# Attention and two MLP layers on one core: other PSUM banks and another order of the weight work at the passage and the seams, and operands at SBUF addresses that are multiples of 512 bytes

## The chip, the cores and the metric

The kernel runs on one core of a Trainium2 chip. Times are device microseconds of an execution. The kernel before took 595.28 us, the median of three runs (594.83 to 597.52).

## The reference

Three stages follow each other. The first is a linear attention with decay, for 2 batches, 8 heads, 768 positions and 64 dimensions a head, by blocks of 64 positions. Its output, as 1536 tokens of 512 numbers, goes through two MLPs with hidden width 2048. All inputs are float32.

```
for b in range(nb):                       # blocks of 64 positions
    intra = (qb @ kb.T * Dmask) @ vb      # Dmask[i, j] = lam ** (i - j) for i >= j, else 0
    inter = (qb * lam_pow) @ kv_state
    out[:, :, sl] = intra + inter
    kv_state = lam_block * kv_state + (kb * rev_pow).T @ vb
h = x @ w_in1;  x = (h * cos(h)) @ w_out1
h = x @ w_in2;  x = (h / (1 + exp(-h))) @ w_out2
```

## The kernel before

**Numbers.** TensorE's matmuls take float32 values rounded to its fp32r form. To keep float32's precision each operand is split into an upper half (`xah`, `gh`, the first half of `win` and `wout`) and a lower half that holds the rest (`xal`, `gl`, the second half), and three matmuls are added: upper by upper, lower weight by upper, upper by lower. `split` (line 120) makes the halves: ScalarE casts the upper one, GpSimd (or the engine given) subtracts it from the value. Weights are read as raw integers, re-biased on ScalarE (`rebias_w`), converted on VectorE (`convert_w`, two instructions), and then split.

**Stages.** Attention runs in chunks of 128 positions (c = 0 to 5) and leaves x transposed: part A holds 512 tokens of each batch, as 2 by 2 quarters with their sums and differences (seven units), part B the rest. Each layer L then has a first product (x by `w_in`, with the nonlinearity) and a second (g by `w_out`), with the intermediate g written to memory (`gd`) and read back.

**First products.** The columns of the weights are taken in pairs j = 0 to 7. For a pair, `sum_w` forms four sums and differences of the weights on GpSimd (VectorE for the second layer's pairs 0 and 1), `split_plain` splits the weights themselves and `split_sums` the sums, and seven products of 6 matmuls (`PRODUCTS`, `product`, line 416) stand for eight. They add up in three PSUM banks: two of `two_banks(i)` (a, b) and one of `one_bank(i)` (d). ScalarE copies bank a to b (`copy_ab`) and b to SBUF (`copy_u`), VectorE forms the other two quarters (`c22`, `c21`). PSUM has eight banks: three pairs `two_banks(0)` to `(2)` and two single ones. In the first layer (`gemm_in_0`, line 510) part A's quads use bank pairs 0 and 1 in turn and part B is a plain product of 24 matmuls with 512 columns (`plain`, line 438) in bank pair 2. In each round j of its loop, TensorE does A's pair j and B's pair j - 1, and the weights of pair j + 1 are prepared by tasks (`task(j, 0)` to `(j, 2)`). In the second layer (`gemm_in_1`, line 577) both parts are quads, B with 256 columns, in bank pairs 2, 0, 1, 2, ..., and tasks are numbered by half a quad.

**Second products.** `gemm_outs` (line 782) walks over items (b, f): b is the block of 512 tokens, f one of 16 slices of the hidden width. One item is 12 matmuls of 512 columns (four output tiles m, three of the split). Blocks 0 and 1 run side by side, block 1 two slices behind, then block 2. Two output tiles of block 0 (m = 0, 1) for f = 0 and 1 are computed within the first product's end, as (0, 1). `load_g` reads g, `prepare` splits it.

**Order.** Each engine executes its instructions in the order of the program, which is written by hand; so does SyncE's queue of loads and stores. A pool's buffer is taken again when its last reader is done.

**Counts from the code.** Matmuls with 512 columns: 2 x 48 x 12 = 1152 in the second products, 2 x 8 x 42 = 672 for part A, 8 x 24 = 192 for part B of the first layer; with 256 columns 8 x 42 = 336 for part B of the second.

**Addresses.** Pools without a side are laid from the bottom of a partition's memory, pools with side "right" from its top. Below the first pool lie 16,512 bytes of the program's own (32 x 512 + 128); `consts` takes 512 and `zeros` 1,024, every later tile a multiple of 512, so that x of part A, g, all weights and all temporaries on the left start at a multiple of 512 plus 128. The right side ends at 229,344 (447 x 512 + 480), and its tiles (q, k, later x of part B, `xbh` and `xbl`) start at a multiple of 512 plus 480. The gap between both sides is 352 bytes. Within a tile, an operand's slices step by 1,024 or 2,048 bytes (x, g) or 512 (weights).

## Time and profile before

| | |
|---|---|
| median of 3 runs | 595.28 us (594.83 to 597.52) |
| profiled execution, in all | 592.26 us |
| its span, first to last instruction | 590.5 us |
| mean granted TensorE clock | 0.99 of 2.4 GHz |
| TensorE busy | 564.3 us (96%) |
| GpSimd, VectorE, ScalarE busy | 350.9, 347.8, 295.7 us |
| attention, to about 55 us | TensorE busy 50.1 of 55.0 us |
| passage and first round, 55 to 93 us | 33.6 of 38.0 |
| first layer, first product, 93 to 182.5 us | 89.4 of 89.5 |
| seam to the second product, 182.5 to 211 us | 20.0 of 28.5 |
| first layer, second product, blocks 0 and 1, to 288.5 us | 77.5 of 77.5 |
| its block 2, to 336 us | 46.6 of 47.5 |
| second layer, first product, to 454.5 us | 114.8 of 118.5 |
| second layer, second product, to 585 us | 130.5 of 130.5 |

A matmul is drawn for longer than the time until the next one starts, since they are pipelined; so a busy TensorE says that it isn't idle, not that it is at its best. Starts are to be read for that.

### The profile page before, as it was taken

The page shows a single profiled execution, that of the slowest core. Times are in us where ns is not written, and L with a number is a line of the kernel's source. Part 1 is how long each engine was busy: PE and PEld are TensorE (multiplying, and loading weights), DVE is VectorE, ACT ScalarE, POOL GpSimd, SP SyncE. Part 2 cuts the span into 40 slices and gives each one's busy share as a digit, 9 for nine tenths or more (in the row PEclk, how much of TensorE's full clock was granted, in tenths as well). Part 3 has the DMA queues.
Part 4 walks back from the last instruction along what each step waited for, and adds up shares of the span by engine and source line. Part 5 has one row for each costly group of instructions (what it writes and reads, how often), then busy time and mean ns, then how long its engine had stood idle before and what let it go on. Part 6 is the DMA issues. An engine that isn't in the chain of part 4 may idle for free.

```text
span 590.5 us, 8374 instructions
## 1 busy us (share of the span) xinstructions
PE 564.3 (96%) x3168; PEld 464.3 (79%) x3168; DVE 347.8 (59%) x355; ACT 295.7 (50%) x440; POOL 350.9 (59%) x261
## 2 busy tenths in 40 slices
PE   7999799999997699999999999999799999999997
PEld 4888587777776488888888788888689888888885
DVE  6689257776677599900499246667666799302001
ACT  4566267777776655310571365666656665201220
POOL 2688635555553699940489338555754699911541
PEclk9999999999998889999999999999999999999999
DMA  9999145445445886740044026455466896205501
GB/s 177 210 233 240 37 141 178 158 153 178 160 166 195 282 329 238 246 144 0 1 143 144 1 72 236 162 182 190 157 241 226 299 319 198 71 1 196 182 15 72
DMA packets 79640, 97.02 MB, mean 164 GB/s; under 512 B 40688, under 2 KB 57072, under 8 KB 79600
## 3 DMA queue, kind: packets, MB, share of 16 engines
q1 hardware_dynamic: 77360, 95.96, 50.8%
q10 hardware_dynamic: 2240, 0.53, 0.5%
q8 instruction: 25, 0.41, 0.3%
q14 instruction: 15, 0.12, 0.1%
HBM read 68.16 MB, written 28.31 MB: 163 GB/s over the span
## 4 chain that ended last, share of the span: by engine, by line
PE 72%; DVE 9%; POOL 6%; issue 4%; DMA 3%; ACT 3%; SPq 1%; ACTq 0%; DVEq 0%; POOLq 0%
PE cab L703 30%; PE cab L429 20%; PE d L429 8%; PE d L703 7%; PE cab L445 6%; DVE xal L122 2%; DVE S L134 2%; POOL win L122 2%; DVE sb L115 1%; DMA q<-in_q_dram 1%; DVE w L116 1%; ACT s L486 1%; DMA v<-in_v_dram 1%; POOL S L134 1%; DMA gf<-gd 1%
## 5 line engine op out<-in xcount | busy, mean ns | idle before, releaser
L122 POOL TENSOR_TENSOR gl<-gf,gh 128x512 fp32r<-128x512 f32 (+1 forms) x68 | 128.6, 1898 | 97.0 <-ACT gh L121 73.3
L703 PE MATMUL cab<-gh,wout 128*128 128x512 f32 x320 | 100.3, 395 | 2.4 <-ACT gh L121 2.4
L703 PE MATMUL cab<-wout,gh 128*128 128x512 f32 x320 | 98.6, 390 | 0.0
L121 ACT CAST gh<-gf 128x512 fp32r<-128x512 f32 (+1 forms) x68 | 53.5, 795 | 85.9 <-DMA out_dram<-o 29.3
L116 DVE SCALAR_TENSOR_TENSOR w<-w,sb 128x512 uint32<-128x512 uint32 x64 | 90.1, 1408 | 9.5 <-ACT w L106 3.2
L429 PE MATMUL cab<-xah,win 128*128 128x512 f32 x320 | 86.9, 394 | 0.2 <-ACT cab L459 0.2
L703 PEld LDWEIGHTS cab<-gh,wout 128*128 128x128 f32 x320 | 61.2, 191 | 15.6 <-ACT gh L121 2.8
L134 POOL TENSOR_TENSOR S<-w 128x256 f32<-128x256 f32 x28 | 30.6, 1091 | 69.6 <-DVE w L116 69.6
L703 PEld LDWEIGHTS cab<-wout,gh 128*128 128x128 f32 x320 | 59.9, 188 | 12.1
L429 PEld LDWEIGHTS cab<-xah,win 128*128 128x128 f32 x320 | 58.9, 188 | 12.8 <-ACT cab L459 0.6
L703 PE MATMUL cab<-gl,wout 128*128 128x512 f32 x160 | 63.7, 398 | 3.9 <-POOL gl L122 3.9
L122 POOL TENSOR_TENSOR wout<-w,wout 128x512 fp32r<-128x512 f32 x32 | 51.4, 1612 | 21.1 <-ACT wout L121 21.1
L115 DVE TENSOR_SCALAR sb<-raw 128x512 uint32<-128x512 uint32 x64 | 61.0, 954 | 3.0 <-DMA raw<-in_moe_w_out_dram 2.0
L703 PE MATMUL cab<-wout,gl 128*128 128x512 f32 x160 | 62.3, 389 | 0.0
L122 POOL TENSOR_TENSOR win<-S,win 128x512 fp32r<-128x512 f32 x32 | 46.5, 1474 | 7.6 <-ACT win L121 7.6
L429 PE MATMUL cab<-xal,win 128*128 128x512 f32 x160 | 49.5, 391 | 0.0
L466 ACT COPY u<-cab 128x512 f32<-128x512 f32 (+1 forms) x48 | 24.6, 513 | 46.9 <-PE cab L429 46.9
L778 DVE COPY o<-cab 128x512 f32<-128x512 f32 x10 | 6.7, 689 | 67.7 <-PE cab L703 65.3
L106 ACT ACTIVATE w<-raw 128x512 f32<-128x512 f32 x64 | 41.9, 671 | 7.3 <-POOL wout L122 3.4
L429 PE MATMUL d<-xah,win 128*128 128x512 f32 x128 | 36.9, 400 | 5.7 <-POOL win L122 2.7
L703 PEld LDWEIGHTS cab<-gl,wout 128*128 128x128 f32 x160 | 30.6, 191 | 11.5 <-POOL gl L122 5.3
L504 DVE TENSOR_TENSOR s<-cab,s 128x1024 f32<-128x1024 f32 (+1 forms) x32 | 34.7, 1084 | 7.0 <-ACT s L486 5.5
(125 smaller groups left out, 976.4 us busy)
## 6 DMA issues: line engine op xcount, KB each, us to landing
gf<-gd SPq DMA_DIRECT2D x46, 512.0 KB, 4.6
gd<-s SPq DMA_DIRECT2D x40, 512.0 KB, 3.1
raw<-in_moe_w_in_dram SPq DMA_DIRECT2D x32, 512.0 KB, 4.3
raw<-in_moe_w_out_dram SPq DMA_DIRECT2D x32, 512.0 KB, 4.6
gd<-s SPq DMA_DIRECT2D x16, 256.0 KB, 2.1
v<-in_v_dram SPq DMA_DIRECT2D x12, 256.0 KB, 6.3
out_dram<-o SPq DMA_DIRECT2D x12, 256.0 KB, 2.1
k<-in_k_dram SPq DMA_DIRECT2D x6, 256.0 KB, 5.7
```

The costliest lines, as they stand in the source:

```text
L106: nc.scalar.activation(w, raw[piece][:, :, 1].bitcast(F32), AF.Prelu, scale=2.0**-112, alpha=-(2.0**32))
L115: nc.vector.tensor_scalar(out=sb, in0=r[:, :, 0], scalar1=2.0**-29, scalar2=7.0, op0=ALU.mult, op1=ALU.min)
L116: nc.vector.scalar_tensor_tensor(out=w, in0=w, scalar=3, in1=sb, op0=ALU.logical_shift_left, op1=ALU.bitwise_or)
L121: nc.scalar.copy(hi, of)
L122: (engine or nc.gpsimd).tensor_tensor(out=lo, in0=of, in1=hi.bitcast(F32), op=ALU.subtract)
L134: engine.tensor_tensor(out=s[:, i], in0=x, in1=y, op=op)
L429: nc.tensor.matmul(Q.banks[bank], w[:, part, wu, kt * P:(kt + 1) * P], x[:, xu, kt, :], start=start and m == 0 and kt == 0, stop=m == 2 an ...
L445: nc.tensor.matmul(Q.cab[:, i], w[:, part, 2 * i + kt // 2, kt % 2 * P:(kt % 2 + 1) * P], x[:, kt, :], start=m == 0 and kt == 0, stop=m == ...
L466: nc.scalar.copy(t, Q.banks["b"])
L504: nc.vector.tensor_tensor(out=t, in0=source(Q, i), in1=t, op=ALU.mult)
L703: nc.tensor.matmul(y[m], x, z, start=f == 0 and n == 0, stop=f == FT - 1 and n == 2)
L778: nc.vector.tensor_copy(o, ys[1, b][2 + m])
```

## The change

It does six things.
- Addresses: an unused tile of 480 bytes at the top of the right side, and `consts` with 96 columns in place of 128. Left tiles then start at 16,512 + 384 + ..., right ones below 228,864: all at multiples of 512. The gap between the sides is gone.
- Passage: the sums of pair 1 and their split go from GpSimd to VectorE and stand earlier; pair 2 is read, converted and summed before A's second quad goes on, and split one task earlier.
- `split_sums` gets the engine of its pair: for the second layer's pairs 0 and 1 it subtracts on VectorE.
- Banks: the last plain product of the first layer uses bank pair 0 in place of 2; blocks 0 and 2 of the second products use pairs 2 and 1 in place of 0 and 1, block 1 pair 0 in place of 2; the second layer's quads go 0, 2, 1 in place of 2, 0, 1.
- Seam: both halves of g for f = 0 and 1 are loaded by single slices one round before the end; block 1's halves are cast around the last sine; and the items of f = 0 and 1 are walked by halves of the output tiles: (1, 0) and (1, 1) with m = 2, 3, then (0, 0) and (0, 1) with m = 2, 3 (in the second layer these first), then (1, 0) and (1, 1) with m = 0, 1. From f = 2 on block 1 runs one slice behind.
- Second layer: the tasks of pair 7 stand one place later, those of the first four output weights two, two, one and two places later; `copy_a` and the sending of block 0 one place later.

```diff
--- before.py
+++ after.py
@@ -65,6 +65,9 @@
...
+    edge = ctx.enter_context(tc.tile_pool(name="edge", bufs=1, side="right"))
+    edge.tile([P, 120], F32, name="edge")
     cpool = ctx.enter_context(tc.tile_pool(name="cpool", bufs=1))
...
@@ -73,7 +76,7 @@
...
-    consts = cpool.tile([P, P], F32, name="consts")
+    consts = cpool.tile([P, 96], F32, name="consts")
     quarter, half_pi = consts[:, 0:1], consts[:, 1:2]
...
@@ -143,12 +146,12 @@
...
-    def split_sums(L, j):
+    def split_sums(L, j, engine=None):
         t = win[L, j]
...
             u = slice(4 + 2 * i, 6 + 2 * i)
-            split(t[:, 0, u], t[:, 1, u], s[:, 2 * i:2 * i + 2])
+            split(t[:, 0, u], t[:, 1, u], s[:, 2 * i:2 * i + 2], engine)
     def split_out(L, f):
...
@@ -163,7 +166,7 @@
...
             lambda: split_plain(L, j),
-            lambda: split_sums(L, j),
+            lambda: split_sums(L, j, engine),
         ]
     def out_tasks(L, f):
@@ -418,7 +421,7 @@
...
             n = Q.j if Q.L == 0 else quads.index(Q)
-            Q.cab = two_banks(n % 2 if Q.L == 0 else (n + 2) % 3)
+            Q.cab = two_banks(n % 2 if Q.L == 0 else (0, 2, 1)[n % 3])
             Q.d = one_bank(n % 2)
...
@@ -438,7 +441,7 @@
     def plain(Q, i):
         if i == 0:
-            Q.cab = two_banks(2)
+            Q.cab = two_banks(2 if Q.j < FP - 1 else 0)
         w, (xh, xl) = win[Q.L, Q.j], xt[Q.L, Q.part]
...
@@ -562,16 +565,15 @@
...
         act_s(Bq, 0)
-        load_halves(0)
         load_g(0, 0, 2)
...
         gemm_out(0, 0, 0, (0, 1))
-        task(FP, 1)
+        prepare_half(0, 1, 0)
         act_sin(Bq, 0)
...
         gemm_out(0, 0, 1, (0, 1))
-        prepare_half(0, 1, 0)
         prepare_half(0, 1, 1)
+        task(FP, 1)
         prepare(0, 0, 2)
     def gemm_in_1(tasks):
@@ -643,10 +645,10 @@
...
-    def load_half(L, f):
+    def load_half(L, i, f):
         t = tpool.tile([P, TB], F32, tag="t2", name="gf", bufs=5)
-        nc.sync.dma_start(out=t, in_=gd[L][f, :, 0:TB])
-        gf[L, "half", 0, f] = t
+        nc.sync.dma_start(out=t, in_=gd[L][f, :, i * TB:(i + 1) * TB])
+        gf[L, "half", i, f] = t
     def load_halves(L):
...
@@ -681,10 +683,10 @@
     def y_tiles(L, b):
...
             if b == 1:
-                t = two_banks(2)
+                t = two_banks(0)
                 ys[L, b] = [t, None, t[:, 0], t[:, 1]] + [one_bank(i) for i in range(2)]
             else:
-                t = [two_banks(i) for i in range(2)]
+                t = [two_banks(i) for i in (2, 1)]
                 ys[L, b] = t + [t[m // 2][:, m % 2] for m in range(4)]
...
@@ -781,11 +783,23 @@
     def gemm_outs(L, tasks):
-        items = [x for f in range(FT + 2) for x in ((0, f), (1, f - 2)) if 0 <= x[1] < FT]
-        items += [(2, f) for f in range(FT)]
-        for b, f in items:
+        lo, hi = (0, 1), (2, 3)
+        items = [(1, 0, hi), (1, 1, hi), (0, 0, hi), (0, 1, hi)]
+        items = (items if L == 0 else items[2:] + items[:2]) + [(1, 0, lo), (1, 1, lo)]
+        items += [(*x, range(4)) for f in range(2, FT + 1) for x in ((0, f), (1, f - 1)) if 2 <= x[1] < FT]
+        items += [(2, f, range(4)) for f in range(FT)]
+        for b, f, ms in items:
             if L == 1 and b == 2 and f >= FT - 2:
                 break
+            if f < 2 and b < 2:
+                gemm_out(L, b, f, ms)
+                if b == 0:
+                    load_g(L, 0, f + 4)
+                elif ms == lo:
+                    prepare(L, 0, f + 2)
+                for x in tasks.get((b, f), []) if ms == hi else []:
+                    x()
+                continue
             if b == 0:
...
@@ -798,7 +812,7 @@
...
                 prepare(L, 2, f + 2)
-            gemm_out(L, b, f, (2, 3) if b == 0 and f < 2 else range(4))
+            gemm_out(L, b, f, ms)
             for x in tasks.get((b, f), []):
...
@@ -895,19 +909,20 @@
...
         split_sums(0, 0)
+        rebias_w(0, 3, 0)
         product(A[0], 1)
...
         att_scores(c, 1, ps_s, "s")
-        rebias_w(0, 3, 0)
         convert_w(0, 3, 0)
         load_next()
-        sum_w(0, 1, nc.gpsimd)
+        sum_w(0, 1, nc.vector)
         product(A[0], 2)
...
         att_intra(c)
+        split_sums(0, 1, nc.vector)
         product(A[0], 6)
...
@@ -923,15 +938,17 @@
...
         c22(A[0])
-        split_sums(0, 1)
+        for i in range(2):
+            rebias_w(0, 4 + i, 0)
+            convert_w(0, 4 + i, 0)
+            load_next()
+        sum_w(0, 2, nc.gpsimd)
         product(A[1], 7)
...
         act_s(A[0], 0)
-        rebias_w(0, 4, 0)
-        rebias_w(0, 5, 0)
         def place(tasks, at_n, fns):
...
@@ -947,25 +964,26 @@
...
                         put((j - 2, 2), *(lambda f=f + i: rebias_w(0, f, 0) for i in range(2)))
-                    for i in range(2):
-                        put((j - 1, 0), lambda f=f + i: convert_w(0, f, 0), load_next)
-                    put((j - 1, 0), lambda j=j: sum_w(0, j, nc.gpsimd))
-                    put((j - 1, 1), lambda j=j: split_plain(0, j))
-                    put((j - 1, 2), lambda j=j: split_sums(0, j))
+                        for i in range(2):
+                            put((j - 1, 0), lambda f=f + i: convert_w(0, f, 0), load_next)
+                        put((j - 1, 0), lambda j=j: sum_w(0, j, nc.gpsimd))
+                    early = j == 2
+                    put((j - 1, 1 - early), lambda j=j: split_plain(0, j))
+                    put((j - 1, 2 - early), lambda j=j: split_sums(0, j))
                 for n, f in ((6, 0), (6, 1), (7, 2), (7, 3)):
...
                     put((n + 1, 1), lambda f=f: split_out(0, f))
-                put((FP - 1, 0), lambda: load_half(0, 0), lambda: load_half(0, 1))
+                put((FP - 1, 0), *(lambda i=i, f=f: load_half(0, i, f) for i in range(2) for f in range(2)))
                 gemm_in_0(tasks)
...
                 for j in range(2, FP):
-                    at_n = min(4 * j - 8, 18)
+                    at_n = min(4 * j - 8, 19)
                     for n, x in zip((0, 1, 2, 2, 3, 4), pair_tasks(L, j)):
                         put(at_n + n, x)
-                for f, n in enumerate((20, 22, 24, 25)):
-                    place(tasks, n - 1, out_tasks(L, f))
-                put(24, *(lambda f=f: load_half(1, f) for f in range(2)))
+                for f, n in enumerate((21, 23, 24, 26)):
+                    place(tasks, n, out_tasks(L, f))
+                put(24, *(lambda f=f: load_half(1, 0, f) for f in range(2)))
                 put(28, lambda: load_halves(1), lambda: prepare_half(1, 0, 0))
...
@@ -977,7 +995,7 @@
...
                 for u in range(2):
-                    tasks.setdefault((1, FT - 3 + u), []).append(lambda u=u: copy_a(u))
+                    put((1, FT - 2), lambda u=u: copy_a(u))
                 tasks.setdefault((1, FT - 1), []).append(lambda: kept.setdefault("a", keep_a()).pop(0)())
...
@@ -986,7 +1004,7 @@
...
                 for m in range(4):
-                    tasks.setdefault((1, FT - 3 + m // 2), []).append(lambda m=m: send(0, m))
+                    put((1, FT - 2 + m // 2), lambda m=m: send(0, m))
                     tasks.setdefault((2, m), []).append(lambda m=m: send(1, m))
...
```

## Rows read from the trace of the kernel before

**Rows 1.** Stretches: us from:to and length; per engine busy us (x count); clock, DMA share, GB/s.

```profile
182.50:211.00 28.50, 20.03 (x69) 15.21 (x68) 21.07 (x19) 17.16 (x23) 17.05 (x10) 0.82 0.69 245
454.50:585.00 130.50, 130.50 (x583) 108.26 (x582) 52.09 (x40) 41.22 (x60) 77.78 (x45) 1.00 0.46 157
```

**Rows 2.** Timeline of TensorE: start, us, engine, line, operation, out<-in, count [idle before].

```profile
270.66 0.39 PE L703 MATMUL cab<-gl,wout 128*128 128x512 f32 x1
...
275.42 0.39 PE L703 MATMUL cab<-gl,wout 128*128 128x512 f32 x1
...
126.55 2.04 PE L445 MATMUL cab<-xbh,win 128*128 128x512 f32 x8
...
129.37 0.86 PE L429 MATMUL cab<-xah,win 128*128 128x512 f32 x3
...
386.12 0.63 PE L429 MATMUL d<-xbh,win 128*128 128x256 f32 x4
...
388.27 0.40 PE L429 MATMUL cab<-xah,win 128*128 128x512 f32 x1
...
206.50 0.63 PE L703 MATMUL cab<-gl,wout 128*128 128x512 f32 x1
...
209.06 0.63 PE L703 MATMUL cab<-gl,wout 128*128 128x512 f32 x1
...
6.13 1.03 PE L822 MATMUL cold<-zeros 128*128 128x512 bf16 x4
```

**Rows 3.** Timeline of the second product's block 2 in the first layer.

```profile
318.05 0.62 ACT L121 CAST gh<-gf 128x512 fp32r<-128x512 f32 x1 [8.39 <-DMA gf<-gd]
...
324.48 2.73 POOL L122 TENSOR_TENSOR win<-S,win 128x512 fp32r<-128x512 f32 x2
...
328.49 0.50 PE L703 MATMUL cab<-gl,wout 128*128 128x512 f32 x1 [0.92 <-POOL gl L122]
```

**Rows 4.** Timeline of a round of the first layer's first product.

```profile
103.93 0.63 PE L429 MATMUL d<-xah,win 128*128 128x512 f32 x2
...
119.46 1.08 PE L429 MATMUL d<-xah,win 128*128 128x512 f32 x4
...
120.17 2.57 POOL L122 TENSOR_TENSOR win<-S,win 128x512 fp32r<-128x512 f32 x2
```

**Rows 5.** Timeline of the passage from attention.

```profile
67.01 1.23 DVE L390 TENSOR_TENSOR xbl<-pso,xbh 128x1024 fp32r<-128x1024 f32 x1 [5.82 <-PE cab L429]
...
70.08 0.73 PE L429 MATMUL d<-xah,win 128*128 128x512 f32 x2 [1.71 <-ACT win L121]
72.13 0.73 PE L429 MATMUL d<-xah,win 128*128 128x512 f32 x2 [1.32 <-POOL win L122]
...
91.78 0.73 PE L429 MATMUL d<-xah,win 128*128 128x512 f32 x2 [1.42 <-POOL win L122]
```

**Rows 6.** Groups by shape, VectorE: count, busy us, mean ns of one, idle before.

```profile
L134 DVE TENSOR_TENSOR S<-w 128x256 f32<-128x256 f32 x4 | 4.4, 1102 | 0.0
```

**Rows 7.** Timeline of the seam in the first layer.

```profile
186.26 3.52 PE L445 MATMUL cab<-xbh,win 128*128 128x512 f32 x8 [3.14 <-DVE s L504]
...
191.41 1.22 DVE L504 TENSOR_TENSOR s<-h,s 128x1024 f32<-128x1024 f32 x1
...
194.70 1.22 DVE L491 SCALAR_TENSOR_TENSOR s<-cab,s 128x1024 f32<-128x1024 f32 x1 [2.07 <-ACT s L482]
...
195.96 1.15 ACT L498 ACTIVATE s<-s,consts 128x1024 f32<-128x1024 f32 x1 [0.27 <-DVE s L491]
...
205.06 0.79 PE L703 MATMUL cab<-gl,wout 128*128 128x512 f32 x1 [2.94 <-POOL gl L122]
```

**Rows 8.** Timeline of the second layer's first product, where TensorE waits.

```profile
416.08 0.67 ACT L106 ACTIVATE w<-raw 128x512 f32<-128x512 f32 x1 [2.12 <-POOL win L122]
...
418.08 0.74 PE L429 MATMUL cab<-xbh,win 128*128 128x256 f32 x4 [1.88 <-ACT cab L459]
...
425.83 0.50 PE L429 MATMUL d<-xah,win 128*128 128x512 f32 x1 [1.21 <-DVE h L474]
```

## The prediction

> **What bounds the kernel now.** I read the stages first: what each engine did in a stretch [rows 1]. In the last product (454.5 to 585 us) TensorE is drawn busy for all 130.5 us and no other engine for more than 78, so there the time is the number of matmuls times their spacing. At the seam between the first layer's two products (182.5 to 211 us) it is busy for 20.0 of 28.5 us, at a granted clock of 0.82. Of the others, TensorE idles a little in the passage out of attention and in the second layer's first product. So two questions decide: how far apart matmuls start, and what is late at the seams.
>
> The spacing comes from the timeline, as the difference of two starts over the matmuls between them [rows 2]. On the left side, where every operand starts 128 bytes behind a multiple of 512: 270.66 to 275.42, 21 matmuls, 0.2267 us each. On the right side (480 behind): 126.55 to 129.37, 12 matmuls, 0.235 us; with 256 columns, 386.12 to 388.27, 18 matmuls, 0.119 us. In a stretch at half clock: 206.50 to 209.06, 6 matmuls, 0.4267 us, which is 512 columns at 1.2 GHz and nothing more. And four bf16 matmuls of 512 columns take 1.03 us with the last drawn at 0.39: 0.213 to 0.215 us, 512 columns at 2.4 GHz. The reader is to see that fp32 loses 0.012 us a matmul at full clock, nothing at half clock, and more on the side that lies at the other offset: a feed that can't quite keep up, and whose price depends on where operands lie.
>
> **The addresses.** Left tiles go from offset 128 to 0, right tiles from 480 to 0. No row of before has an operand there. The bounds for a 512-column matmul are 0.215 (the bf16 row) and 0.2267 (nothing gained), and upwards 0.238 (the right side's 0.235 and a little). I take 0.215: the excess differs by offset and vanishes where the feed has time, so it looks like split fetches, and an aligned one should not split. 256 columns: 0.119 now, 0.109 if half of 0.215 plus a rounding, 0.1135 as half of the left's spacing.
> - First layer's second product, blocks 0 and 1: 28 of its steps stand behind the seam, 12 matmuls each, 336 x 0.0117 = 3.9 us, all on the path: TensorE is drawn busy for all of that stretch.
> - Its block 2: 192 matmuls, 2.2 us, of which I take 0.3. There the path is not TensorE's: at 328.49 it waits 0.92 for a lower half that stood behind two weight splits on GpSimd, and at 318.05 ScalarE had waited 8.39 for a load [rows 3] whose issue stands in SyncE's queue behind a weight load that waits for VectorE. The change moves four of those weight splits (`split_sums` for the second layer's pairs 0 and 1) from GpSimd to VectorE: that frees the first wait and lengthens the second. Bounds: 3.5 gained (2.2, the 0.92 and a restart) to 2.6 lost (two subtractions on VectorE at the 1.28 that GpSimd needs).
> - Second layer's first product: 336 x 0.0117 + 336 x 0.010 = 7.3 us, of which 6.5, since some copies out of PSUM will be waited for.
> - Second layer's second product: 576 x 0.0117 = 6.7 us, less its tail: 6.6 [rows 1].
> - First layer's first product: two things are nearly equally late [rows 4]. From the end of the plain product (103.93, where the next begins) over ScalarE, VectorE and GpSimd to the split weights two rounds on (120.17 + 2.57 = 122.74) it takes 18.8 us; from there to the end of the following plain product TensorE needs 12.2 us (52 matmuls; 103.93 + 2 x 15.53 = 135.0). A chain of 31.0 us over two rounds is 15.5 a round, the 15.53 of the trace (119.46 - 103.93) [rows 4]. Faster matmuls shorten only the 12.2, by 24 x 0.020 + 28 x 0.012 = 0.8: (18.8 + 11.4) / 2 = 15.1 a round, where TensorE alone would need 14.2. Five rounds: 2.1 us, not 6.
> - Attention's small matmuls: no row shows what an address costs them. Taken as nothing; at most 2 us, some 700 at a quarter of 0.0117.
>
> Together 19.4 us.
>
> **The passage.** TensorE waits for split weights at 70.08 (1.71), 72.13 (1.32) and 91.78 (1.42) [rows 5]; with the 0.16 by which a matmul is drawn longer than its slot and a slow first start after each, 5.2 us. The change sums and splits pair 1 on VectorE and starts pair 2 earlier. Added on VectorE: four sums, 1.1 us each where VectorE did such before [rows 6], and two subtractions; removed from GpSimd as much. VectorE's cover is its idle 5.82 us before 67.01 [rows 5]; it would start at 61.2, as now, and end at 61.2 + 4.4 + about 1 = 66.6, before the 68.2 (70.08 - 1.71 - 0.16) at which TensorE gets there. Moved up with pair 2 are two reads, two conversions and their two weight loads in SyncE's queue; ScalarE and VectorE wait for TensorE there. I take all of it: 5.2; if the sums take twice as long, 2 of it are lost. Behind it the loop [rows 4] takes over, which the figure above contains.
>
> **The seam in the first layer.** In those 28.5 us [rows 1] TensorE does 24 plain matmuls (x 0.235) and 44 others (x 0.2267): 15.6 us. So 12.9 are lost: the wait for the plain product's bank, 3.14 at 186.26, until VectorE has read it; two waits for the halves of the second product's input, 2.94 the longest [rows 7]; and a clock at half in between (18 matmuls x 0.2). The change gives the last plain product bank pair 0, which is free, so the first wait goes, and loads block 1's halves early. What is late next: block 1's step 1 stands early in the new order, and its upper half is cast behind `act_sin` of the last quarter on ScalarE. That is VectorE's end at 191.41 + 1.22, then `act_s` 1.22, the sine 1.15, the cast 0.62: 195.6 us, the lower half 1.3 later [rows 3, 7]. TensorE is there at 192.7 (183.0 + 24 x 0.235 + 18 x 0.2267). I charge 4.3 us for that and 1.0 for clock: gain 7.6. Bounds: 10 (the helpers lead more than I think) and 4 (the clock falls again).
>
> In the second layer every bank is merely renamed (0 and 2 swapped); no cost. In its first product TensorE loses 1.88 and 1.21 and some restarts, 4 us, while a read of pair 7 on ScalarE waits 2.12 for its buffer with `copy_ab` behind it [rows 8]. Pair 7 and the first output tiles go back by a place or two: 2.0 of 4, between none and all.
>
> **Sum.** 19.4 + 5.2 + 7.6 + 2.0 = 34.2 us. The profiled execution took 592.26 us in all (span 590.5); 34.2 less is 558.1. The median of the runs lies 3.0 above it, so for the median **561.1 us**.
>
> **What a page says against it.** On the right side of SBUF operands cost more than on the left, 0.235 against 0.2267 [rows 2]. The Trainium skill (SBUF — State Buffer, Door 1: The DMA port swizzle) has a line of 16 bytes there, and a penalty for crossing to a new one. 128 and 480 are both multiples of 16, so by that page neither side pays and the change of address gives nothing; the trace disagrees for the right side, and for the left it doesn't tell. That case is the first rival.
>
> **Rivals.**
> - *The left side's 0.2267 is the price of fp32 as such*; only the right side improves, to the left's rate. Then the passage 5.2, the seam 7.6, the stalls 2.0, 336 x (0.119 - 0.1135) = 1.8 and 0.3 in the loop: 16.9, **578**. For it: the spacing on the left is the same for every operand, bank and weight. Against it: the half clock shows no fixed price.
> - *The rate falls, but the helpers take over*: the first-product stages keep their time, the seam loses 3 more: 34.2 - 6.5 - 2.1 - 3 = 22.6, **573**. For it: what is late there now [rows 3, 4]. Against it: in the last product the helpers are busy for at most 78 of 130.5 us [rows 1].
> - *Slower: data and weights now start at the same offset, and the two reads meet.* Price: spacing. It decides from 0.235 us: 14.8 us of seams over 1824 left matmuls are 0.008 each. At 0.238, the slowest that I allow, 1824 x 0.0113 + 192 x 0.003 - 14.8 = 6.4 slower: **602**. For it: offset 0 is not in the trace. Against it: on the left both reads share their offset already and are the faster ones.
>
> **How the numbers follow.** Forecast 0.50, first rival 0.27, second 0.13, slower 0.07, and 0.03 for a mixture that cancels. The forecast alone is 553 to 569 (the seam's, the passage's and block 2's bounds); with the two faster rivals the range is 553 to 582. About 0.5% is what a measurement here can tell from no change: faster 0.89, within 0.04, slower 0.07.
>
> **What would show it.** Starts 0.215 to 0.217 apart in the last product, which should take some 124 us instead of 130.5, confirm the addresses; 0.2267 there makes it the first rival. No wait of TensorE for `win` before 80 us confirms the passage. No wait for VectorE's `s` at the last plain product, and one for block 1's `gh` behind the sine, confirm the seam. Rounds of 15.1 us confirm the loop; 14.3 would mean that its chain is shorter than I read. Wrong would be above all a spacing between 0.22 and 0.225, or the small matmuls of attention gaining.

## The result and the profile after

The changed kernel takes **575.55 us** (574.46 to 576.00); the kernel before took 595.06 beside it, and the ratio is 0.967 (0.963 to 0.971). The range of the forecast, 553 to 582, holds that; its centre, 561.1, lies 14 us too low. What came is close to the first rival, at 578: the spacing of matmuls on the left side did not move, while the passage, the seam and the second layer's stalls gave 5.3, 4.85 and 3.3 us, where 5.2, 7.6 and 2.0 were charged.

The spans of the two profiled executions differ by 16.9 us, 590.5 and 573.6. Between the starts of the first or last matmuls of the stages it divides like this (us):

| stage | before | after | gained | forecast |
|---|---|---|---|---|
| attention, up to the first product's first matmul | 54.84 | 52.80 | 2.04 | 0, at most 2 |
| passage, up to the first plain product | 23.77 | 20.16 | 3.61 | 5.2, with part of the next line |
| loop of the first product | 104.11 | 101.53 | 2.58 | 2.1, beside that part |
| seam, up to the 100th matmul of the second product | 41.24 | 36.39 | 4.85 | 7.6 |
| rest of the second product | 109.41 | 109.00 | 0.41 | 3.9 and 0.3 |
| second layer, first product | 125.23 | 121.91 | 3.32 | 6.5 and 2.0 |
| second layer, second product | 127.76 | 127.76 | 0.00 | 6.6 |
| end | 4.11 | 4.00 | 0.11 | 0 |

First the two stretches of [rows 1], shifted by as much as their stage starts earlier (from:to, length, busy us of each engine with its count, granted clock, DMA share, GB/s):

```profile
174.30:202.80 28.50, 23.98 (x91) 18.30 (x90) 22.86 (x18) 16.37 (x23) 17.54 (x11) 0.88 0.74 260
437.60:568.10 130.50, 130.50 (x582) 107.95 (x581) 52.63 (x40) 40.83 (x60) 79.36 (x46) 1.00 0.46 156
```

In the seam TensorE gets through 91 matmuls where it did 69, and the clock is 0.88 instead of 0.82. In the last product it does 582 where it did 583: not one matmul more. The spacings say why. TensorE's timeline of the kernel after, answering [rows 2]:

```profile
261.67 0.39 PE L705 MATMUL d<-gl,wout 128*128 128x512 f32 x1
...
267.79 0.39 PE L705 MATMUL cab<-gl,wout 128*128 128x512 f32 x1
...
118.61 1.98 PE L448 MATMUL cab<-xbh,win 128*128 128x512 f32 x8
...
121.33 0.39 PE L432 MATMUL cab<-xah,win 128*128 128x512 f32 x1
...
384.24 0.40 PE L432 MATMUL cab<-xbl,win 128*128 128x256 f32 x2
...
385.68 0.40 PE L432 MATMUL cab<-xbl,win 128*128 128x256 f32 x2
```

Left side: 27 matmuls from 261.67 to 267.79, 0.2267 us each, as before. Right side: 12 from 118.61 to 121.33, 0.2267, where it was 0.235. With 256 columns: 12 from 384.24 to 385.68, 0.120, where it was 0.119. So the new addresses changed the spacing in one place only, the plain matmuls of the first layer.

The passage has no wait left. The wait of 0.92 in block 2 [rows 3] is still there:

```profile
312.28 0.50 PE L705 MATMUL cab<-gl,wout 128*128 128x512 f32 x1 [0.81 <-POOL gl L125]
```

### The profile page after: what moved, and what is told of

Read it like the earlier page. It is cut to its first block, busy times and chain, and to the rows that moved or that the text cites. A ratio compares the mean times of both kernels' runs of the same rounds, so it can differ in the third digit from the quotient of the medians.

```text
span 573.6 us, 8373 instructions
## 1 busy us (share of the span) xinstructions
PE 559.7 (98%) x3168; PEld 463.4 (81%) x3168; DVE 354.2 (62%) x365; ACT 295.0 (51%) x440; POOL 337.9 (59%) x251
## 4 chain that ended last, share of the span: by engine, by line
PE 77%; DVE 5%; POOL 5%; DMA 4%; issue 3%; ACT 3%; ACTq 0%; SPq 0%; POOLq 0%; DVEq 0%
PE cab L705 36%; PE cab L432 18%; PE d L705 7%; PE d L432 7%; POOL win L125 3%; PE pso L353 2%; PE cab L448 2%; DMA q<-in_q_dram 2%; PE psc L331 2%; POOL S L137 2%; PE pt L249 2%; POOL gl L125 1%; DVE s L494 1%; DVE s L507 1%; DMA raw<-in_moe_w_in_dram 1%
## 5 line engine op out<-in xcount | busy, mean ns | idle before, releaser
L125 POOL TENSOR_TENSOR gl<-gf,gh 128x512 fp32r<-128x512 f32 (+1 forms) x68 | 131.0, 1933 | 95.7 <-ACT gh L124 70.3
L119 DVE SCALAR_TENSOR_TENSOR w<-w,sb 128x512 uint32<-128x512 uint32 x64 | 79.0, 1234 | 9.2 <-ACT w L109 3.0
L118 DVE TENSOR_SCALAR sb<-raw 128x512 uint32<-128x512 uint32 x64 | 73.1, 1143 | 2.8 <-DMA raw<-in_moe_w_out_dram 1.8
L137 POOL TENSOR_TENSOR S<-w 128x256 f32<-128x256 f32 x26 | 27.2, 1046 | 70.5 <-DVE w L119 70.5
L125 POOL TENSOR_TENSOR wout<-w,wout 128x512 fp32r<-128x512 f32 x32 | 49.9, 1566 | 19.5 <-ACT wout L124 19.5
L125 POOL TENSOR_TENSOR win<-w,win 128x512 fp32r<-128x512 f32 (+1 forms) x32 | 39.3, 1247 | 2.7 <-ACT win L124 2.7
L124 ACT CAST wout<-w 128x512 fp32r<-128x512 f32 x32 | 19.6, 620 | 37.2 <-DVE w L119 37.2
L125 POOL TENSOR_TENSOR win<-S,win 128x512 fp32r<-128x512 f32 x26 | 36.4, 1423 | 3.7 <-ACT win L124 3.7
```

The costliest lines, as they stand in the source:

```text
L118: nc.vector.tensor_scalar(out=sb, in0=r[:, :, 0], scalar1=2.0**-29, scalar2=7.0, op0=ALU.mult, op1=ALU.min)
L119: nc.vector.scalar_tensor_tensor(out=w, in0=w, scalar=3, in1=sb, op0=ALU.logical_shift_left, op1=ALU.bitwise_or)
L124: nc.scalar.copy(hi, of)
L125: (engine or nc.gpsimd).tensor_tensor(out=lo, in0=of, in1=hi.bitcast(F32), op=ALU.subtract)
L137: engine.tensor_tensor(out=s[:, i], in0=x, in1=y, op=op)
```

## Experiments

### The addresses alone

```diff
+    edge = ctx.enter_context(tc.tile_pool(name="edge", bufs=1, side="right"))
+    edge.tile([P, 120], F32, name="edge")
-    consts = cpool.tile([P, P], F32, name="consts")
+    consts = cpool.tile([P, 96], F32, name="consts")
```

> The kernel before with the new addresses alone: left tiles at a multiple of 512 bytes instead of 128 behind one, right tiles at one instead of 480 behind. The forecast charged 19.4 us to this part, so by it this kernel would stand near 576. Theory now: 0.2267 us is what a 512-column fp32 matmul costs at full clock wherever its operands lie on the left, and only the right side's 0.235 falls to 0.2267; the rounds of the first product keep their 15.5 us, since something other than TensorE sets them. Then the plain matmuls of the passage and the seam give 48 x 0.008 = 0.4, and the 2.0 us by which attention ended earlier in the changed kernel (54.84 to 52.80) belong to the addresses: 2.4 in all, near 593. If attention's 2.0 came from the new order of instructions instead: 0.4, near 595.

Measured: 592.35 beside 595.04, ratio 0.9957 (0.9935 to 0.998), so 2.6 us, from 1.2 to 3.9. That refutes the 19.4 of the forecast. In its trace attention ends at 52.59, 2.2 us earlier, and the left matmuls stand 0.2267 apart as ever.

Then the left side alone:

```diff
-    consts = cpool.tile([P, P], F32, name="consts")
+    consts = cpool.tile([P, 96], F32, name="consts")
```

> The kernel before with only the left tiles moved, from 128 to 0 behind a multiple of 512; q, k, the decayed k and the input tiles of the third block stay on the right at 480. No theory gives the left matmuls a gain (0.2267 stays). What it tells is which side attention's 2.0 us belong to: if to the left (v, the transposed tiles), the first matmul of the first product starts 2.0 us earlier and the time is 2.0 lower; if to the right (q, k), nothing moves by more than 0.3 us.

Measured: 592.29, ratio 0.9952 (0.993 to 0.9975), and in the trace attention ends at 55.17: nothing is gained there, and the span is 591.1. The two readings don't agree. By the runs the left side alone gives as much as both; by the traces attention's gain belongs to the right. On attention the traces agree among themselves: in the eight kernels here whose right side lies at a multiple of 512 it ended between 52.6 and 53.8, in the six that left it at 480, or put it at 448, between 54.8 and 55.4. No run moves the right side alone. How the 2.6 us of the runs divide stays open; that they are not 19 doesn't.

The transfers suggest where attention's time comes from. Windows of the first 12 us (last column GB/s) of four kernels: before, left side moved, both moved, and right side at 448 (an experiment below):

```profile
0.00:12.00 12.00, 8.04 (x59) 4.22 (x61) 6.95 (x10) 5.92 (x12) 2.67 (x9) 1.00 0.91 167
```

```profile
0.00:12.00 12.00, 9.41 (x62) 5.02 (x62) 6.95 (x10) 5.98 (x12) 2.68 (x9) 1.00 0.82 171
```

```profile
0.00:12.00 12.00, 9.09 (x78) 5.29 (x78) 7.00 (x11) 6.15 (x12) 2.67 (x9) 1.00 0.85 191
```

```profile
0.00:12.00 12.00, 9.57 (x52) 4.97 (x54) 6.95 (x10) 5.68 (x12) 2.67 (x9) 1.00 0.90 167
```

The loads arrive at 191 GB/s instead of 167 when all their tiles start at a multiple of 512. The packets of 256 bytes show which: of those in the first 50 us 97% took 18 ns with both sides moved (35,751 of 36,735), 87% with the left alone (30,555 of 35,155) and 56% before (19,470 of 34,816), where most of the others took 19 to 29. So the loads gain on both sides, v's on the left too. That this makes attention's 2 us is argued, not shown: TensorE's waits for loads in attention fall from 3.5 us to 2.3, but with the right side at 448 they are 2.1, and attention gains nothing there.

The Trainium skill (DMA: Bandwidth & Descriptors, How a descriptor splits into AXI transactions) says that a transaction which reads must start on a multiple of 256 bytes, so that a descriptor which starts elsewhere fetches bytes that it doesn't use and pays for them. The pieces of q and k are rows of 64 fp32, 256 bytes. The trace is in line with it, 480 and 448 give 167 and 0 gives 191. But the Trainium skill tells it of reading, and what moved here are the addresses written in SBUF; no run here shows whether the same holds for them.

Why did the runs with both sides moved not gain attention's 2 us more than those with the left alone? In the profiled execution the passage took them back; whether it did in the others isn't shown. Windows from 62 to 80 us, before and with both sides moved:

```profile
62.00:80.00 18.00, 14.96 (x87) 11.66 (x86) 5.70 (x6) 8.96 (x13) 7.17 (x8) 1.00 0.09 28
```

```profile
62.00:80.00 18.00, 14.96 (x52) 11.23 (x51) 5.16 (x6) 8.52 (x12) 4.86 (x4) 0.81 0.00 0
```

and TensorE's timeline of the second of them:

```profile
67.81 0.73 PE L431 MATMUL d<-xah,win 128*128 128x512 f32 x2 [1.71 <-ACT win L123]
69.87 1.22 PE L431 MATMUL d<-xah,win 128*128 128x512 f32 x2 [1.33 <-POOL win L124]
...
76.00 0.63 PE L431 MATMUL d<-xal,win 128*128 128x512 f32 x2
```

The waits are those of [rows 5], 1.71 and 1.33; but here the clock falls to half behind them, 0.4267 a matmul until 76.00, and 14 matmuls lose 3.0 us. That happened in three of the six traces that have these waits, and not in the trace of before that the forecast was made from.

### Other offsets

```diff
-    consts = cpool.tile([P, P], F32, name="consts")
+    consts = cpool.tile([P, 136], F32, name="consts")
```

> The kernel before with every left tile 32 bytes further: 160 behind a multiple of 512 instead of 128; the right side stays. If a moving operand off a multiple of 64 costs 0.235, the 1824 matmuls of 512 columns that read the left side take 0.008 more each: some 14 us less what helpers hide in the first product's loop, 604 to 609. If the offset is without effect on the left, nothing.

Measured: 594.97 beside 594.77, ratio 0.9993 (0.9965 to 1.0021). Nothing: the left matmuls stand 0.2267 apart at 160 as at 128 and at 0. And though the right side was not touched, its plain matmuls came closer together.

```diff
+    edge = ctx.enter_context(tc.tile_pool(name="edge", bufs=1, side="right"))
+    edge.tile([P, 8], F32, name="edge")
```

> The kernel before with every right tile 32 bytes lower: 448 behind a multiple of 512 instead of 480, a multiple of 64 but of no larger power of two. If a multiple of 64 is enough, the right side's matmuls take 0.2267, and attention ends 1.9 us earlier, as with 0: near 592.5, as the kernel with the new addresses alone. If it has to be a multiple of 512: 0.235 or attention as before. The two may part: matmuls and transfers need not want the same.

Measured: 594.80, ratio 0.9992 (0.9971 to 1.0013); attention ends at 55.05, at 167 GB/s. A multiple of 64 is not enough for the transfers. TensorE's timeline of a plain product, first with the left side at 160 and the right at 480, then with 128 and 448:

```profile
126.67 2.01 PE L445 MATMUL cab<-xbh,win 128*128 128x512 f32 x8
...
129.44 1.10 PE L429 MATMUL cab<-xah,win 128*128 128x512 f32 x4
```

```profile
129.59 2.01 PE L447 MATMUL cab<-xbh,win 128*128 128x512 f32 x8
...
132.35 0.86 PE L431 MATMUL cab<-xah,win 128*128 128x512 f32 x3
```

2.77 and 2.76 us for 12: 0.231 and 0.230. In the first the right side is where it was (480) and only the weights, on the left, have moved; so the price of 0.235 isn't a property of the moving operand's address alone. In both, right less left is 320 bytes.

### The cost by itself

```diff
+            px = slabs(L)[0].rearrange("p s a c -> p (s a c)")
+            pb = one_bank(0)
+            for _ in range(16):
+                nc.tensor.matmul(pb[0:128, 0:512], px[:, 4096:4224], px[:, 0:512], start=True, stop=True)
...
```

> The changed kernel with 21 series of 16 matmuls behind its last step, all into one bank, with the slab of the second product as moving operand (512 columns of fp32 from byte 0, 16, 32, 64, 128, 256 and 480 behind a multiple of 512) and as weights (from 0, 32, 128 and 480), then fewer columns (256 and 384), weights of 64 and 32 columns, half the partitions, and bf16. Theory: the kernel's own spacings, 0.2267 on the left at 128 and at 0, 0.235 on the right at 480, come from whether the moving operand starts on a multiple of 64 bytes: 0.2267 from 0, 64, 128 and 256, 0.235 from 16, 32 and 480; and 0.2267 is 512 columns at 2.4 GHz and 0.0133 for each fp32 matmul, so 384 columns take 0.173 and 256 take 0.120, and bf16 0.2155. Rival: it is the weights' offset, or the two together; then the series with weights at 32 or 480 differ. The forecast's view, that an operand at a multiple of 512 is fed at 0.215, needs 0.215 in the first series. If the weights' load sets the 0.0133, it falls with 64 and 32 columns of weights.

The timeline of TensorE behind the last step, in one execution; a series' spacing is the start of the next one less its own, by 16:

```profile
570.87 3.79 PE L826 MATMUL d<-gh 128*128 128x512 f32 x16
574.50 3.87 PE L828 MATMUL d<-gh 128*128 128x512 f32 x16
578.20 3.90 PE L830 MATMUL d<-gh 128*128 128x512 f32 x16
581.94 3.82 PE L832 MATMUL d<-gh 128*128 128x512 f32 x16
585.60 3.88 PE L834 MATMUL d<-gh 128*128 128x512 f32 x16
589.32 3.81 PE L836 MATMUL d<-gh 128*128 128x512 f32 x16
592.97 3.90 PE L838 MATMUL d<-gh 128*128 128x512 f32 x16
596.70 3.88 PE L840 MATMUL d<-gh 128*128 128x512 f32 x16
600.42 3.88 PE L842 MATMUL d<-gh 128*128 128x512 f32 x16
604.14 3.81 PE L844 MATMUL d<-gh 128*128 128x512 f32 x16
607.79 2.07 PE L846 MATMUL d<-gh 128*128 128x256 f32 x16
609.69 2.05 PE L848 MATMUL d<-gh 128*128 128x256 f32 x16
611.58 2.06 PE L850 MATMUL d<-gh 128*128 128x256 f32 x16
613.48 2.96 PE L852 MATMUL d<-gh 128*128 128x384 f32 x16
616.28 3.83 PE L854 MATMUL d<-gh 128*64 128x512 f32 x16
619.96 3.87 PE L856 MATMUL d<-gh 128*32 128x512 f32 x16
...
627.61 3.63 PE L860 MATMUL d<-zeros 128*128 128x512 bf16 x16
631.07 3.62 PE L862 MATMUL d<-zeros 128*128 128x512 bf16 x16
```

With both operands at 0 the spacing is (574.50 - 570.87) / 16 = 0.227, and 0.2267 between its own starts. L828 to L838 keep the weights at 0 and move the other operand: 0.231 at 16 bytes, 0.234 at 32, 0.229 at 64, 0.232 at 128, 0.228 at 256, 0.233 at 480. L840 and L842 keep that one at 0 and move the weights by 32 and 128: 0.233 and 0.232. In L844 both lie at 480: 0.228. So my theory of a multiple of 64 bytes falls (128 is one and costs 0.232, 480 is none and costs 0.228 with weights beside it): what shows is the **difference** of the two offsets. Equal, 0.227 to 0.228; unequal, 0.228 to 0.234.

The single starts within a series say more than its mean. In L826 to L844 the matmuls at equal offsets, and at 256 apart, stand 0.2267 apart after at most five of them; at 16, 32, 64, 128 and 480 apart they vary between 0.225 and 0.241 to the end. So a difference of 256 costs nothing that lasts. Two more series, L864 and L866, change the weights with each matmul as the kernel does: at equal offsets the last five stand 0.2267 apart, with 480 between them all take 0.233. The plain matmuls of the kernels agree, on the mean at full clock: 0.2267 without a difference (eight traces), 0.230 at 320, 0.234 at 352 and at 480. This explains the left side, which never paid at 128, 160 or 0: weights and moving operand shared their offset there all along, and the right side was the one that differed, by 352.

Nothing came to 0.215 but bf16 (L860: 3.46 / 16 = 0.216). fp32 takes 0.119 at 256 columns, 0.175 at 384 and 0.2267 at 512 on the mean of a series, and 0.120, 0.173 and 0.2267 at its end: each 128 columns take 0.053, which is the 2.4 GHz, and some 0.013 stand on top of every matmul, whatever its columns. With 256 columns the offsets cost nothing either: 0.118 at 32 and at 480 apart (L848, L850), where equal ones take 0.119. The 0.013 doesn't fall with 64 columns of weights (L854: 0.230), so the length of the weights' load doesn't set it. Why that series, at equal offsets, takes 0.230 and not 0.227 is open, so equality is not the whole rule.

### The passage alone

```diff
+        rebias_w(0, 3, 0)
         product(A[0], 1)
...
-        sum_w(0, 1, nc.gpsimd)
+        sum_w(0, 1, nc.vector)
...
+        split_sums(0, 1, nc.vector)
...
-        split_sums(0, 1)
+        for i in range(2):
+            rebias_w(0, 4 + i, 0)
+            convert_w(0, 4 + i, 0)
+            load_next()
+        sum_w(0, 2, nc.gpsimd)
```

> The kernel before with the passage's new weight order alone: pair 1 summed and split on VectorE, its second read and the split of pair 0 earlier, pair 2 converted and summed at the passage. Theory: the waits at 70.08 (1.71), 72.13 (1.32) and 91.78 (1.42) go with their restarts, 5.2 us, near 590, whatever the addresses. Rival: the helpers only get there in time because attention ended 2.0 us earlier or its operands were aligned; then one of the three waits stays, 3 to 4 us.

Measured: 588.38 beside 595.04, ratio 0.9881 (0.9842 to 0.992). In the trace the passage takes 20.16 us, as in the changed kernel, and the loop 102.05, 2.1 less: 5.7 together, with attention and addresses as before. The theory holds, and the rival falls. The runs gave more than the 5.2, 6.7 by the medians (4.8 to 9.4 by the interval); the half clock that these waits brought in some executions, shown above, went with them, but that it makes the difference is argued, not shown.

### The seam alone

```diff
-            Q.cab = two_banks(2)
+            Q.cab = two_banks(2 if Q.j < FP - 1 else 0)
...
-        items = [x for f in range(FT + 2) for x in ((0, f), (1, f - 2)) if 0 <= x[1] < FT]
+        items = [(1, 0, hi), (1, 1, hi), (0, 0, hi), (0, 1, hi)]
...
```

> The kernel before with the banks, the order of items and the loads of the seam alone. Theory: the wait of 3.14 for the plain product's bank goes, a wait for block 1's upper half behind the sine takes its place, and the seam loses 4.6 us (the 4.84 of the changed kernel less 24 x 0.008 for the addresses), near 590.5; renaming banks in the second layer gives 0. Rival: the renamed banks or the later copies out of PSUM move other stages by over 0.5 us.

Measured: 589.40, ratio 0.9899 (0.9858 to 0.994); the seam takes 36.53 instead of 41.24, 4.7 less, and no stage of the second layer moved by over 0.1. As expected; only the passage took 1.6 more than in the kernel before, at half clock behind its waits. The next experiment takes its new wait.

### The cast ahead of the sine

```diff
         prepare_half(0, 1, 0)
+        prepare_half(0, 1, 1)
         act_sin(Bq, 0)
...
         gemm_out(0, 0, 1, (0, 1))
-        prepare_half(0, 1, 1)
```

> The changed kernel with one cast moved: block 1's second upper half (step 1) is cast on ScalarE ahead of the last quarter's sine, not behind it. Theory: the wait of 3.84 and the 0.54 behind it go, and with them part of the 6.8 us at half clock (up to 2.8), 4.4 to 7.2. Less what is late next: step 2's input, whose load waits for a buffer that VectorE frees at 186.4, is split at 195.7 at the earliest, and TensorE would be there at about 193, so some 2.5 come back: 2 to 5 us net, 571 to 574. Rival: the half clock stays because the new wait brings it back, then 2 or less.

The timeline of the changed kernel's seam:

```profile
183.01 1.48 DVE L118 TENSOR_SCALAR sb<-raw 128x512 uint32<-128x512 uint32 x1
184.26 0.50 PE L705 MATMUL d<-gl,wout 128*128 128x512 f32 x1 [0.53 <-POOL gl L125]
...
185.20 1.22 DVE L507 TENSOR_TENSOR s<-h,s 128x1024 f32<-128x1024 f32 x1
186.34 1.22 DVE L494 SCALAR_TENSOR_TENSOR s<-cab,s 128x1024 f32<-128x1024 f32 x1
...
187.59 1.15 ACT L501 ACTIVATE s<-s,consts 128x1024 f32<-128x1024 f32 x1 [4.74 <-DVE s L494]
188.65 0.60 ACT L124 CAST gh<-gf 128x512 fp32r<-128x512 f32 x1
189.30 1.22 PE L705 MATMUL d<-gh,wout 128*128 128x512 f32 x2 [3.84 <-ACT gh L124]
```

and with the cast moved, TensorE's waits:

```profile
184.42 0.50 PE L705 MATMUL d<-gl,wout 128*128 128x512 f32 x1 [0.32 <-POOL gl L125]
191.21 0.70 PE L705 MATMUL cab<-gh,wout 128*128 128x512 f32 x2 [1.42 <-DVE s L507]
196.23 0.50 PE L705 MATMUL cab<-gl,wout 128*128 128x512 f32 x1 [1.61 <-POOL gl L125]
```

Measured: 571.94 beside 594.56, ratio 0.9622 (0.9592 to 0.9652). By the medians that is 3.6 us under the changed kernel, though the intervals of the two ratios still touch; in the trace the seam takes 32.44, 3.95 less. The wait of 3.84 goes, with it the stretch at half clock (the clock from 172 to 210 us is 1.00, in the changed kernel 0.91), and two shorter waits come: the one for step 2 that was expected, and one for the bank of the last plain product, behind VectorE.

### A read moved in the loop

```diff
-                        put((j - 2, 2), *(lambda f=f + i: rebias_w(0, f, 0) for i in range(2)))
+                        put((j - 2, 1), lambda f=f: rebias_w(0, f, 0))
+                        put((j - 2, 2), lambda f=f: rebias_w(0, f + 1, 0))
```

> The changed kernel with one of the two weight reads of each round of the first product's loop moved on ScalarE, from behind the casts of the sums to ahead of them, where ScalarE idles. Theory: the round of 15.5 us is a circle of the helpers alone: GpSimd's four sums (3.74), ScalarE's last cast, two reads of 0.56 and the plain product's conversion to integers (about 2.85), eight to nine steps of VectorE (8.8), and again the sums. One read less in it takes 0.56 off the circle, TensorE's wait of 0.42 with its 0.11 goes, and four rounds give 2.1 us, near 573.5; rounds of 15.0. Rival, the forecast's: the chain lies half on TensorE, over two rounds; then 0.28 a round, 1.1 us. Rival: the moved read waits for its load and nothing is gained.

The circle, in the changed kernel's timeline of one round:

```profile
112.62 1.22 DVE L494 SCALAR_TENSOR_TENSOR s<-cab,s 128x1024 f32<-128x1024 f32 x1 [3.87 <-ACT s L485]
...
121.53 1.59 POOL L137 TENSOR_TENSOR S<-w 128x256 f32<-128x256 f32 x1 [6.72 <-DVE w L119]
...
125.35 0.62 ACT L124 CAST win<-S 128x512 fp32r<-128x512 f32 x1 [0.77 <-POOL S L137]
125.88 1.22 ACT L109 ACTIVATE w<-raw 128x512 f32<-128x512 f32 x2
126.99 2.12 ACT L485 ACTIVATE s<-cab,consts 128x1024 int32<-128x1024 f32 x2
128.14 1.23 DVE L494 SCALAR_TENSOR_TENSOR s<-cab,s 128x1024 f32<-128x1024 f32 x1 [3.88 <-ACT s L485]
```

From 112.62 to 128.14 it closes, 15.52 us, over VectorE, GpSimd and ScalarE; TensorE isn't in it. Measured with one read less in it: 573.42, ratio 0.9634 (0.9605 to 0.9663), by the medians 2.1 us under the changed kernel as expected, though the intervals of the two ratios overlap. The loop takes 100.03 instead of 101.53, a round 15.14 instead of 15.44 on the mean of four, and TensorE, which waited 1.1 us there in all, is drawn busy without a gap. The circle was the bound; the rest of the 0.56 could not be had because TensorE is the bound from there on (66 matmuls x 0.2267 = 15.0 a round). The forecast's rival fits the stage's 1.5 no worse; it is the closed circle in the rows that decides against it, and the kernel with the addresses alone: its plain matmuls took 0.2 us a round less (24 x 0.008), of which half should have shown by that rival, and its rounds were 15.52 on the mean of five, where they were 15.53.

### The second layer's tasks back

```diff
-                    at_n = min(4 * j - 8, 19)
+                    at_n = min(4 * j - 8, 18)
...
-                for f, n in enumerate((21, 23, 24, 26)):
-                    place(tasks, n, out_tasks(L, f))
+                for f, n in enumerate((20, 22, 24, 25)):
+                    place(tasks, n - 1, out_tasks(L, f))
```

> The changed kernel with the weight work of the second layer's first product at its old places: pair 7 and the first four output tiles a place or two earlier. Theory: the stalls of 2.04, 1.37 and 0.36 that are gone from that stage in the changed kernel come back, 3.3 us, near 579. Rival: they went with the renamed banks or the addresses, and nothing comes back.

Measured: 578.69, ratio 0.9726 (0.9692 to 0.9759), and 125.23 us for that stage, exactly the time of before. Its first wait is back:

```profile
404.46 0.74 PE L432 MATMUL cab<-xbh,win 128*128 128x256 f32 x4 [1.86 <-ACT cab L462]
```

That is 2.0 with its restart. Behind it 12 matmuls run at half clock and lose some 1.6, and the second wait of the kernel before, 1.21 [rows 8], doesn't come. So one wait and the half clock took as long here as two waits at full clock did before; the shift takes away both.

On their own the four parts, addresses 2.7, passage 6.7, seam 5.6 and this one 3.1, make 18.1 of the 19.5 us by the medians.

### Combined

```diff
+        load_half(0, 1, 2)
         act_g(old, 1)
         act_n(Bq, 0)
         act_s(Bq, 0)
-        load_g(0, 0, 2)
...
         prepare_half(0, 1, 0)
+        prepare_half(0, 1, 1)
+        prepare_half(0, 0, 2)
         act_sin(Bq, 0)
...
```

> The changed kernel with the cast ahead of the sine, the moved read of the loop, and step 2 of block 0 loaded as two halves early, into small buffers that are free, with its first half cast ahead of the sine too. Theory: cast 4.4 to 7.2 with nothing late behind it, loop 2.1: 6.5 to 9 us below the changed kernel, 566 to 569. Rival: the bank that the last quarter's VectorE steps free at 190 is late next, 1 us or less of that.

Measured: 570.76 (570.24 to 571.29), ratio 0.9594 (0.9566 to 0.9622): better than both kernels, but 4.8 us under the changed one instead of 6.5 to 9. The wait for step 2 is gone, and the bank that the rival named is late. TensorE's wait, and a step of VectorE ahead of it, drawn out to 2.32 us, behind two conversions (1.50 and 1.59 in their longer steps):

```profile
185.06 2.32 DVE L507 TENSOR_TENSOR s<-h,s 128x1024 f32<-128x1024 f32 x1
...
191.09 0.70 PE L706 MATMUL cab<-gh,wout 128*128 128x512 f32 x2 [2.52 <-DVE s L507]
```

So the conversions were moved behind the steps that free the bank:

```diff
-        task(FP, 0)
         plain(Bq, 1)
...
         act_s(Bq, 0)
+        first, second = tasks[FP, 0][:2], tasks[FP, 0][2:]
+        for x in first:
+            x()
...
         act_g(Bq, 0)
+        for x in second:
+            x()
```

> The combined kernel with the two weight conversions at the seam moved on VectorE, one behind the step that the sine waits for, one behind the last multiplication. Theory: in the combined kernel TensorE waits 2.68 us for the bank of the last plain product, since two conversions of 1.11, drawn out to 2 and 3 beside GpSimd, stand on VectorE ahead of the steps that free it; without them the bank is free before TensorE comes, 2.7 less, near 568. Rival: the output weights of steps 2 and 3 come too late instead, and the 2.7 return as a wait for them.

Measured: 570.03 (569.22 to 571.95), ratio 0.9577 (0.9542 to 0.9612). The wait for the bank is gone, and 1.9 of its 2.7 us return as a wait for the lower half of step 3, whose cast now stands on ScalarE behind a weight read that waits for its load. The seam takes 32.35 (33.02 in the combined kernel, 32.44 with the cast alone): each wait taken away there uncovers the next within 3 us. The two kernels can't be told apart by their intervals.

## Why the forecast was right and wrong

**The addresses** are the step that failed, 2.6 us by the runs instead of 19.4. "I take 0.215: the excess differs by offset and vanishes where the feed has time, so it looks like split fetches." Two readings were wrong in it. That the right side paid more than the left [rows 2] said that some of the right's excess hangs on addresses, not that all of the left's does; the series show 0.2267 as the floor of fp32 with both operands at a multiple of 512. And the half clock shows no fixed price because it hides one: 0.013 us a matmul is there at full clock for any number of columns, and not at 0.4267. The 0.119 for 256 columns stood in [rows 2] and half of 0.215 is 0.1075: its excess of 0.0115 was as large as that of 512 columns on the left, which is what a fixed price looks like. I read it as a multiple of the offset's price instead. The right side fell from 0.235 to the left's 0.2267, as the first rival had it, and not to 0.215. What the series show stood in the argument against the slower rival: on the left both reads share their offset already and are the faster ones.

Of its parts: the second layer's second product, charged with 6.6, gained 0.0; its first product's 6.5 and the 3.9 of the second product's blocks likewise. The range of 0.215 to 0.2267 was named, and the wrong end taken.

**Attention**, taken as nothing, at most 2, gained 2.04. I asked what an address costs its matmuls, not what it costs its transfers, though TensorE waits for loads there.

**The loop** was given half of what the faster matmuls save, over two rounds. It gained next to none of it: rounds of 15.53 before and, but for the first two, which the passage's order shortens (15.21 and 15.23 with that alone), 15.51 to 15.55 after, and TensorE's waits grew from about 0.15 to 0.42 by what it saved. The chain of [rows 4] is right in its members but it isn't half on TensorE: it closes over helpers within one round. The second rival, which keeps the time of the first products, was right for this stage, for another reason than a rate that falls.

**The passage** was right, place and size: 5.2 forecast, 3.61 and the 1.69 of the third wait with its restart measured. Its VectorE was oversized: three of the four sums took 0.41 to 0.43 and one 1.51, where all were charged with 1.1 [rows 6], and from the first sum to the last split it took 4.0 us, where 5.4 was charged.

**The seam** was right in mechanism: no wait for the bank, and one for block 1's upper half behind the sine, 3.84. The term mis-sized is what is left: 5.3 us were charged for the new wait and the clock; the rows give 4.0 with its restart, 0.9 for the lower half behind it, 0.8 for a wait at 184.26 that the forecast hadn't, and 11 matmuls at half clock, 2.3. Together 8.0, so 4.85 gained instead of 7.6; the bounds, 4 to 10, held.

**The second layer's stalls**: 2.0 of 4 forecast, 3.3 gained.

**The total** came within the range for a reason that the chances had at 0.27: the largest term, 19.4 of 34.2, was wrong, and the range held the result because it had been drawn around the first rival too. That the spans differ by just that rival's 16.9 is luck. Against the first rival's 16.9 stand 2.0 from attention and 1.3 more stalls, less 2.8 at the seam and 1.8 from 256 columns, which gave nothing: 15.6; the loop's first round, block 2 and the end bring it to the 16.9 of the two spans. The median fell by 19.5, 2.6 more than the spans. The constant of 3.0 between the profiled execution and the median was not a constant: the profiled execution of before was one in which the passage kept its clock. That this makes the 2.6 is not shown.

## What to carry to other kernels

A price that differs between two addresses shows that part of it hangs on them; before the rest is charged to addresses too, look for the same price at another size, where a fixed cost per instruction keeps its size and a rate doesn't. Before a loop's time is divided between engines, follow its chain until it closes: if it comes back to its own start without the engine that you speed up, that engine's gain becomes its wait. And a wait of TensorE is to be priced with the half clock that can follow it: behind the waits of 1.3 to 3.8 us here it cost up to as much again in some executions and nothing in others.

## What the runs showed of the hardware

- The spacing of fp32 matmuls with 512 columns hangs on where weights and moving operand lie relative to each other: 0.2267 at equal offsets and at 256 bytes apart once a series has settled, 0.229 to 0.234 at 16, 32, 64, 128 and 480 apart, 0.235 on the right side of the kernel before. With 256 columns no such price shows (0.118 to 0.120). The Trainium skill (SBUF — State Buffer, Who interferes with whom) gives TensorE two independent read ports, one for each, and says that it never waits on anyone; the series differ from that by up to 0.007 us a matmul, and what the two reads share is open.
- fp32 costs some 0.013 us a matmul over its columns at 2.4 GHz (0.119, 0.175, 0.2267), bf16 0.003 (0.216).
- Loads into tiles that start at a multiple of 512 bytes ran at 188 to 192 GB/s in the first 12 us, into tiles of which some or all lay at 128, 160, 448 or 480 at 164 to 171. Their packets of 256 bytes took 18 ns in the first case, and often 19 to 29 in the others.
- VectorE's conversions are drawn out when GpSimd works beside them. In the rows of the changed kernel's seam above one took 1.48 us. Of the 64, the 27 that ran without GpSimd took 0.41 to 0.43; of the 37 beside it half took over 1.5, up to 2.53. The same page and section of the Trainium skill has the two engines share a pair of ports that one of them holds for a whole instruction; the trace agrees.
